# Delta rule scan: which engine spreads W and copies the state, from chunk 9 and after the last solve

## The chip, the cores and the metric

One core of a Trainium2 chip runs the whole program. The metric is the device time of one execution in microseconds; the lower, the better. TensorE multiplies matrices into PSUM, VectorE (DVE in the rows) and ScalarE (ACT) read PSUM and write SBUF, GpSimd (POOL) fills tiles and scatters rows, SyncE (SP) issues most transfers. Each engine runs its own instructions in the order in which the program issues them, and waits for another engine through semaphores.

## The reference, cut to what matters

Three stages follow each other. The first is a delta rule over 4 batches of 8 heads with 768 tokens of 48 elements; the second sends each of the 3072 resulting rows of 384 to one of 8 experts, the third is a feed-forward layer with a squared ReLU. The change lies in the first stage alone:

```python
k_n = k / (norm(k) + 1e-06)
state = zeros((B, H, D, D))
for t in range(S):
    y[:, :, t] = q_t @ state
    v_old = k_n_t @ state
    state = state + beta_t * outer(k_n_t, v_t - v_old)
```

## The kernel before, in words

**Chunks.** The 768 tokens are cut into 24 chunks of 32 (`s`, `NS = 24`), which run one after the other in the loop of `attention()`, because each needs the state that the one before left. All 32 pairs of batch and head are worked at once, as two halves `hq` of four heads times four batches. Four chunks form a group `g` of six.

**A chunk.** For each half, TensorE adds the values (`mmV`) and the keys times the state (`mm1K`) in the bank `CH[hq]`. `U(s)` spreads the result into a block-diagonal tile `Ub[hq]`: half 0 on VectorE by one multiplication of 128x768 with a mask (`blocks`), half 1 on ScalarE by four copies of 32x192. Then come the queries times the state (`mm1Q`), the transposes of the last chunk's output rows (`xrt`, copied by ScalarE), and `W`: TensorE multiplies `Ub` with the inverted triangle `TTl[g]` into columns 256 to 448 of `CH[hq]`, and the result is spread, negated, into the block-diagonal `Wb[hq]`. Half 0 goes to ScalarE as four copies (L358), half 1 to VectorE as one `blocks` (L326). `xlog` makes the router's logits. `dS` (L364) multiplies the raw keys with `Wb[hq]` into the state bank `SP_[hq]`, for half 0 and then for half 1, eight matmuls each; every one of them reads all 128 partitions of `Wb[hq]`. ScalarE copies the state of each half to `Sb[hq]` in two parts of 48x384 (L374, four a chunk). `PW` (L396) makes the output rows from both `Wb`, and ScalarE copies them to `XG` (L408).

**Order.** Nothing is scheduled by a tool: every engine gets its instructions in the order of the Python code (`manual_schedule`). The triangles are solved on VectorE, in `lanes(g)`, as a stream of some 100 short operations for each group (L271, L279, and at the end the transposes L284). `fill()` deals these out at three places of a chunk by a budget; a stream leaves `streams` when its last operation is issued. Streams 0 to 5 are due by chunks 0, 4, 8, 12, 16 and 20. The router of the rows (`route`) also runs on VectorE: `R[0]` finds the expert of each row (L446 to L466, one-hot at L455), `R[1]` are TensorE's rank counts (L460, L463), `R[2]` the slots on VectorE (L471 to L487), after which GpSimd scatters the rows (L490). For chunks 20 and 21 the router's three parts are issued at the very end of chunks 21 and 22, so `R[1]` stands on TensorE ahead of `mmV` and `mm1K` of the next chunk. In chunks 21 to 23 VectorE also rounds the first expert's weights (`pre1`, L636), after `W` and ahead of `xlog`.

**After the loop** the last rows are routed, the rows of the first expert are gathered, and the experts start, whose matmuls fill TensorE to the end.

Of the kernel before, what the change touches and what calls it, by code (L numbers as in the profile page):

```python
# [13 lines left out]
AF = mybir.ActivationFunctionType  # L14
# [8 lines left out]
def kernel(  # L23
# [17 lines left out]
    V, G, A, PE = nc.vector, nc.gpsimd, nc.scalar, nc.tensor  # L41
    NT, DM = out.shape
    D = k2.shape[-1]
    NS, C = kq.shape[0], kq.shape[-1]
# [70 lines left out]
    CH = [pp.tile([128, 512], F32, name=f"ch{i}") for i in range(2)]  # L115
    SP_ = [pp.tile([128, 512], F32, name=f"sp{i}") for i in range(2)]
# [6 lines left out]
    Wb = [wp.tile([128, 4, 4, 48], F32, name=f"Wb{i}") for i in range(2)]  # L123
    Sb = [wp.tile([128, 4, 2, 2, 48], F32, name=f"Sb{i}") for i in range(2)]
# [69 lines left out]
    def masked(g, b):  # L194
        a = PL2[g][:, b].rearrange("p s c j -> p (s c) j")
        V.tensor_tensor(a, a, mask.unsqueeze(1).broadcast_to([128, 8, C]), ALU.mult)
# [103 lines left out]
    def mmV(s, hq):  # L300

        g, i = divmod(s, 4)
        PE.matmul(
            CH[hq][:, 0:192],
            ident,
            vV[g][:, i, 4 * hq : 4 * hq + 4].rearrange("p a e -> p (a e)"),
            start=True,
            stop=s == 0,
            skip_group_check=True,
        )  # L310

    def mm1K(s, hq):
        for m in range(2):
            for b in range(4):
                PE.matmul(
                    CH[hq][C * b : C * b + C, m * 96 : m * 96 + 96],
                    KQ[s][0][:, hq * 2 + m, b],
                    Sb[hq][:, b, m].rearrange("p a e -> p (a e)"),
                    start=False,
                    stop=True,  # L320
                    skip_group_check=True,
                )

    def blocks(o, w, n):

        V.tensor_tensor(  # L326
            o,
            w.rearrange("p (x e) -> p x e", e=D).unsqueeze(2).broadcast_to([128, 4, 4, D]),
            blk[:, n].unsqueeze(1).unsqueeze(3).broadcast_to([128, 4, 4, D]),
            ALU.mult,  # L330
        )

    def U(s):
        blocks(Ub[0], CH[0][:, 0:192], 0)
        for b in range(4):
            A.activation(
                Ub[1][C * b : C * b + C, :, b, :],
                CH[1][C * b : C * b + C, 0:192].rearrange("p (a e) -> p a e", a=4),
                AF.Copy,
            )  # L340

    def W(s, hq):
        g, i = divmod(s, 4)
        for f in range(4):
            PE.matmul(
                CH[hq][C * f : C * f + C, 256:448],
                TTl[g][:, i * 8 + hq * 4 + f],
                Ub[hq][:, f].rearrange("p b e -> p (b e)"),
                start=True,
                stop=True,  # L350
            )
        if hq:
            blocks(Wb[1], CH[1][:, 256:448], 1)
            return
        for f in range(4):
            o = Wb[0][C * f : C * f + C, :, f, :]
            w = CH[0][C * f : C * f + C, 256:448].rearrange("p (b e) -> p b e", b=4)
            A.activation(o, w, AF.Copy, scale=-1.0)  # L358

    def dS(s, hq):  # L360
        g, i = divmod(s, 4)
        for b in range(4):
            for par in range(2):
                PE.matmul(  # L364
                    SP_[hq][64 * par : 64 * par + D, b * 96 : b * 96 + 96],
                    kL2[g][:, i, b * 2 + hq],
                    Wb[hq].rearrange("p b (m r) e -> p b r m e", r=2)[:, b, par],
                    start=(s == 0 and b == 0),
                    stop=(s == NS - 2),
                    skip_group_check=True,  # L370
                )
        for par in range(2):
            r = 64 * par
            A.activation(  # L374
                Sb[hq][r : r + D, :, :, par, :],
                SP_[hq][r : r + D, 0:384].rearrange("p (b m e) -> p b m e", b=4, m=2),
                AF.Copy,
            )

    def mm1Q(s):  # L380
        for p in range(4):
# [261 lines left out]
    def attention():  # L643
        streams, route_q = deque(), deque()
# [30 lines left out]
        def fill(now, part):  # L675

            nonlocal budget, lent
            pace = max(need(now), 8.0 if now < 3 else 6.6 if now < 16 else 0)
            budget += pace * part
            while streams and budget > 0 or route_q:  # L680
                if streams and budget > 0:
                    a, b = streams[0], streams[1] if len(streams) > 1 else None
                    most = pace * (due(a.g) - now)
                    c = a.pop()
                    budget -= c
                    lent += c * (most / max(a.left + c, 0.1) - 1)
                    if b is None or now < b.since or not a.ops:
                        lent = 0.0
                    if lent > 0:
                        c = b.pop()  # L690
                        lent -= c
                        budget -= c
                if route_q:
                    route_q.popleft()()
            if not streams:
                budget = 0.0
# [76 lines left out]
        for s in range(NS):  # L773
            g, i = divmod(s, 4)
            last = g == NG - 1
            while s not in ready:
                streams[0].pop()
            if s:
                mmV(s, 0)
                mmV(s, 1)  # L780
                mm1K(s, 0)
                mm1K(s, 1)
            U(s)
            fill(s, 0.25)
            if s:
                mm1Q(s)
            if s > 0:
                xT = xrt(s - 1)
            while streams and streams[0].g <= g:
                streams[0].pop()  # L790
            W(s, 0)
            W(s, 1)
            if s == NS - 1:
                lows.pop(0)()
            if s == 0:
                for b in range(4):
                    masked(0, b)
            for _ in range(2 if s > 1 else 1):
                if ahead < min(15 if s < 3 else 18 if s < 4 else NS, s + 15):
                    gram(ahead)  # L800
                    ahead += 1
            if scats and s >= E:
                drain(route_q)
                scats.pop(0)()
            fill(s + 0.25, 0.4)
            if s == NS - 4:
                first_x()
            if s >= NS - 3:
                pre1(s - NS + 3, False)
            if scats and s >= NS - 10:  # L810
                scats.pop(0)()
            if R is not None and s in (6, 10, 14, 17, 19):
                drain(route_q)
                R[1]()
                queue(R[2])
                scats += R[3]
            if s > 0:
                xlog(s - 1, xT)
                if i == 0 or s == 18:
                    R = route(g, 0, 2) if i else route(g - 1, 2 if s == 20 else 0, 4)  # L820
                    R[0][0]()
                    queue(R[0][1:])
                    if last and i == 0:
                        drain(route_q)
            if s + 1 < NS:
                dS(s, 0)
                dS(s, 1)
            if s == NS - 1:
                R = route(NG - 1, 2, 3)
                for o in R[0]:  # L830
                    o()
            PW(s)
            if last and i == 0:
                R[1]()
                queue(R[2])
                scats += R[3]
            if s <= E:
                padding(s)
            if s == 0:
                for n in range(15, 18):  # L840
                    load_kq(n)
            if i == 3 and g + 2 < NG:
                load_v(g + 2)
                load_k2(g + 2)
            if s % 3 == 2:
                for n in range(s + 16, min(s + 19, NS)):
                    load_kq(n)
            while ahead // 4 - 1 > made:
                made += 1
                streams.append(Stream(made, s + 1.6))  # L850
            fill(s + 0.65, 0.35)
            if s in (15, 17, 20):
                pre1((15, 17, 20).index(s), True)
            if s in (NS - 3, NS - 2):
                R = route(g, s - NS + 3, s - NS + 4)
                for o in R[0] + [R[1]] + R[2]:
                    o()
                scats += R[3]
# [560 lines left out]
```

## Time and profile before

| What | Value |
|---|---|
| Time, median of 3 runs | 946.1 us (945.6 to 953.18) |
| The profiled execution: its own time, and its span | 945.33 us, 943.6 us |
| PE busy | 874.4 us (93%) |
| DVE busy | 619.3 us (66%) |
| ACT busy | 449.0 us (48%) |
| POOL busy | 102.8 us (11%) |
| Mean granted TensorE clock | 0.962 |

The chunk loop takes the span from about 51 us to 257 us. The busy shares are means over the whole span, and stages with different limits lie in it. In the page's row of 40 slices VectorE stands at 8 or 9 tenths from 24 to 236 us and mostly lower in the third stage. A chunk is dated here by the end of its work on ScalarE, the copy to `XG` (L408).

### The profile page before, as it was taken

How to read it: one execution, taken by the hardware profiler on the slowest of the kernel's cores; microseconds unless marked ns; L12 is line 12 of the kernel's file. 1: busy time of each engine (PE TensorE's matmuls, PEld its weight loads, DVE VectorE, ACT ScalarE, POOL GpSimd, SP SyncE). 2: the span in 40 equal slices, each digit the busy share in tenths (PEclk: the TensorE clock that was granted, in tenths of full speed). 3: DMA queues.
4: the chain of work that ended last, by engine and by line, in shares of the span. 5: the costliest groups of instructions: out<-in, count | busy, mean ns of one | idle time of the engine just before them, and what ended most of it. 6: DMA issues, size and time to landing. Idle time of an engine off the chain costs nothing.

```text
span 943.6 us, 22357 instructions
## 1 busy us (share of the span) xinstructions
PE 874.4 (93%) x8859; PEld 787.2 (83%) x8859; DVE 619.3 (66%) x1655; ACT 449.0 (48%) x1115; POOL 102.8 (11%) x144
## 2 busy tenths in 40 slices
PE   4668889999899899998999799999999999999998
PEld 2446667667688788897987699999999999999998
DVE  6998899998668898888888592615243342516150
ACT  2245767667744666465646381514233332424150
POOL 3002013212211122212211200000000000000000
PEclk7587999999999999999999899999999999999999
DMA  8785866141245677477666550101010202020000
GB/s 332 238 264 195 241 182 186 69 148 68 75 154 167 227 259 257 151 237 241 215 216 208 154 143 17 34 17 34 17 34 9 42 9 43 9 43 1 26 1 25
DMA packets 98850, 117.80 MB, mean 125 GB/s; under 512 B 56147, under 2 KB 75706, under 8 KB 98736
## 3 DMA queue, kind: packets, MB, share of 16 engines
q1 hardware_dynamic: 90288, 89.37, 31.1%
q0 software_dynamic: 8288, 26.87, 7.7%
q8 instruction: 75, 1.23, 0.5%
q14 instruction: 39, 0.32, 0.1%
q10 hardware_dynamic: 160, 0.01, 0.0%
HBM read 84.12 MB, written 32.89 MB: 124 GB/s over the span
## 4 chain that ended last, share of the span: by engine, by line
PE 51%; issue 4%; DVE 3%; ACT 2%; DMA 1%; POOL 0%; POOLq 0%; DVEq 0%; ACTq 0%
PE gp L1129 7%; PE gp L1131 7%; PE gp L1130 7%; PE xp L1129 4%; PE xp L1131 4%; PE xp L1130 4%; PE yp L1129 3%; PE yp L1131 3%; PE yp L1130 3%; PE sp L1131 3%; PE sp L1130 3%; PE sp L1129 3%; DMA wscr<-t2k 1%; DVE wb L581 1%; ACT junk L907 1%
## 5 line engine op out<-in xcount | busy, mean ns | idle before, releaser
L1328 DVE TENSOR_TENSOR t4k<-t2k 128x384 f32<-128x384 f32 x128 | 71.3, 557 | 196.6 <-ACT t2k L1327 193.7
L1129 PE MATMUL xp<-wb,hh 128*128 128x384 f32 x184 | 62.1, 338 | 0.0
L279 DVE TENSOR_TENSOR TL<-TL,tmp 128x135 f32<-128x135 f32 (+15 forms) x186 | 60.9, 337 | 1.8
L1131 PE MATMUL xp<-wb,hl 128*128 128x384 f32 x184 | 61.9, 336 | 0.0
L1130 PE MATMUL xp<-wb,hh 128*128 128x384 f32 x184 | 61.8, 336 | 0.0
L271 DVE TENSOR_TENSOR tmp<-AL,TL 128x135 f32<-128x135 f32 (+15 forms) x186 | 60.5, 337 | 1.6
L374 ACT ACTIVATE Sb<-sp 48x384 f32<-48x384 f32 x92 | 44.7, 485 | 26.1 <-PE sp L364 24.4
L1129 PE MATMUL yp<-xh,W 128*128 128x384 f32 (+1 forms) x156 | 52.9, 339 | 1.2 <-DVE hl L1222 1.2
L1129 PE MATMUL sp<-xh,W 128*128 128x384 f32 (+1 forms) x156 | 52.8, 338 | 0.7 <-DVE hl L1222 0.5
L1131 PE MATMUL sp<-xh,W 128*128 128x384 f32 (+1 forms) x156 | 52.8, 338 | 0.5 <-DVE W L581 0.5
L1130 PE MATMUL sp<-xl,W 128*128 128x384 f32 (+1 forms) x156 | 52.7, 338 | 0.2 <-DVE xl L958 0.2
L1131 PE MATMUL yp<-xh,W 128*128 128x384 f32 (+1 forms) x156 | 52.6, 337 | 0.0
L1130 PE MATMUL yp<-xl,W 128*128 128x384 f32 (+1 forms) x156 | 52.5, 337 | 0.0
L1129 PE MATMUL gp<-wb,hh 128*128 128x384 f32 x152 | 51.4, 338 | 0.0
L1131 PE MATMUL gp<-wb,hl 128*128 128x384 f32 x152 | 51.1, 336 | 0.0
L1130 PE MATMUL gp<-wb,hh 128*128 128x384 f32 x152 | 51.1, 336 | 0.0
L1272 POOL DMA_INDIRECT x<-y,rows x32 | 34.3, 1072 | 131.5 <-ACT y L1269 74.0
L1129 PE MATMUL gp<-xh,W 128*128 128x384 f32 (+1 forms) x144 | 48.6, 337 | 0.0
L1131 PE MATMUL gp<-xh,W 128*128 128x384 f32 (+1 forms) x144 | 48.5, 337 | 0.0
L1130 PE MATMUL gp<-xl,W 128*128 128x384 f32 (+1 forms) x144 | 48.4, 336 | 0.0
L364 PE MATMUL sp<-Wb,kL 128*48 128x96 f32 x736 | 44.4, 268 | 1.3 <-DVE Wb L326 0.9
L1351 ACT ACTIVATE y<-gp 128x384 f32<-128x384 f32 x12 | 5.9, 492 | 82.8 <-PE gp L1131 82.8
(327 smaller groups left out, 2483.4 us busy)
## 6 DMA issues: line engine op xcount, KB each, us to landing
W<-in_moe_w_dram SPq DMA_DIRECT2D x42, 256.0 KB, 8.1
hb<-in_moe_w_dram SPq DMA_DIRECT2D x24, 384.0 KB, 5.3
t4k<-in_moe_w_in_dram SPq DMA_DIRECT2D x12, 512.0 KB, 4.0
t4k<-in_moe_w_out_dram SPq DMA_DIRECT2D x16, 384.0 KB, 3.3
W<-wscr SPq DMA_DIRECT2D x16, 384.0 KB, 3.9
W<-in_kq_dram SPq DMA_DIRECT2D x11, 512.0 KB, 6.4
xs<-padrow POOLq DMA_DIRECT2D x8, 693.0 KB, 7.8
xe<-xs SPq DMA_DIRECT2D x8, 594.0 KB, 7.5
```

The costliest lines, as they stand in the source:

```text
L271: V.tensor_tensor(tv[0], AL[:, j, j + 1 :].unsqueeze(1).broadcast_to([128, n, m]), T[:, :n, j : j + 1].broadcast_to([128, n, m]), ALU.mult,)
L279: V.tensor_tensor(T[:, : j + 1, j + 1 :], T[:, : j + 1, j + 1 :], tv[0], ALU.add)
L364: PE.matmul(SP_[hq][64 * par : 64 * par + D, b * 96 : b * 96 + 96], kL2[g][:, i, b * 2 + hq], Wb[hq].rearrange("p b (m r) e -> p b r m e", ...
L374: A.activation(Sb[hq][r : r + D, :, :, par, :], SP_[hq][r : r + D, 0:384].rearrange("p (b m e) -> p b m e", b=4, m=2), AF.Copy,)
L581: El.tensor_tensor(part(wt, 1, c, n), raw, hi.bitcast(F32), ALU.subtract)
L907: add(lambda t=t: A.activation(junk[:p], x[:, t, 0:DM], AF.Square, accum_out=ss[:, t : t + 1]))
L1129: PE.matmul(ps, hs, rh, start=first, stop=False)
L1130: PE.matmul(ps, hs, rl, start=False, stop=False)
L1131: PE.matmul(ps, ls, rh, start=False, stop=last)
L1272: to_x2 = lambda n=n, t=t, y=y, rows_e=rows_e: G.indirect_dma_start(out=x2, out_offset=bass.IndirectOffsetOnAxis(ap=rows_e[:n, t : t + 1]. ...
L1328: V.tensor_tensor(s2, r, r, ALU.mult)
L1351: A.activation(y, ps[:, :DM], AF.Copy)
```

## The change

`W` and `dS` take a flag. `solved` is true when no stream of solve operations is left at the point of `W`.

- Chunks 0 to 8: as before in which engine does what.
- From chunk 9, while a solve is left: both halves of W are spread by ScalarE, four copies each.
- Where no solve is left: both halves of W are spread by VectorE, one `blocks` each, and the state of half 1 is copied by VectorE (two copies of 48x384) in place of ScalarE.

```diff
-    def W(s, hq):
+    def W(s, hq, dve):
 ...
-        if hq:
-            blocks(Wb[1], CH[1][:, 256:448], 1)
+        if dve:
+            blocks(Wb[hq], CH[hq][:, 256:448], 1)
             return
         for f in range(4):
-            o = Wb[0][C * f : C * f + C, :, f, :]
-            w = CH[0][C * f : C * f + C, 256:448].rearrange("p (b e) -> p b e", b=4)
+            o = Wb[hq][C * f : C * f + C, :, f, :]
+            w = CH[hq][C * f : C * f + C, 256:448].rearrange("p (b e) -> p b e", b=4)
             A.activation(o, w, AF.Copy, scale=-1.0)
-    def dS(s, hq):
+    def dS(s, hq, dve):
 ...
         for par in range(2):
             r = 64 * par
-            A.activation(
-                Sb[hq][r : r + D, :, :, par, :],
-                SP_[hq][r : r + D, 0:384].rearrange("p (b m e) -> p b m e", b=4, m=2),
-                AF.Copy,
-            )
+            o = Sb[hq][r : r + D, :, :, par, :]
+            d = SP_[hq][r : r + D, 0:384].rearrange("p (b m e) -> p b m e", b=4, m=2)
+            if dve:
+                V.tensor_copy(o, d)
+            else:
+                A.activation(o, d, AF.Copy)
...
-            W(s, 0)
-            W(s, 1)
+            solved = not streams
+            W(s, 0, solved)
+            W(s, 1, solved or s < 9)
...
-                dS(s, 0)
-                dS(s, 1)
+                dS(s, 0, False)
+                dS(s, 1, solved)
```

## Rows read from the trace of the kernel before

**Rows 1.** Stretch view, five chunks: width, busy PE, PEld, DVE, ACT, POOL, clock

```profile
165.58:175.34 9.76, 8.11 (x139) 5.93 (x139) 9.61 (x33) 5.50 (x14) 3.45 (x5) 0.83 0.25 96
175.34:183.47 8.13, 7.74 (x145) 5.63 (x144) 8.13 (x34) 5.38 (x14) 1.95 (x2) 1.00 0.21 77
190.64:199.65 9.01, 7.98 (x139) 6.15 (x139) 8.94 (x32) 5.50 (x15) 1.95 (x2) 0.81 0.47 141
199.65:207.75 8.10, 8.04 (x145) 5.77 (x144) 7.07 (x19) 5.38 (x14) 1.05 (x2) 1.00 0.68 249
222.63:229.82 7.19, 7.19 (x147) 5.36 (x146) 7.00 (x22) 5.38 (x14) 2.25 (x3) 1.00 0.34 118
```

**Rows 2.** Timeline of chunk 19: start, length, instruction, idle before and releaser

```profile
225.43 1.34 ACT L358 ACTIVATE Wb<-ch 32x192 f32<-32x192 f32 x4
226.09 0.95 DVE L326 TENSOR_TENSOR Wb<-ch,blk 128x768 f32<-128x768 f32 x1
226.82 1.32 PEld L364 LDWEIGHTS sp<-Wb,kL 128*48 128x48 f32 x30 [0.18 <-ACT Wb L358]
227.78 2.02 ACT L374 ACTIVATE Sb<-sp 48x384 f32<-48x384 f32 x4 [1.01 <-PE sp L364]
228.27 0.48 PEld L396 LDWEIGHTS yp<-Wb,PL 128*32 128x32 f32 x16
229.91 0.65 PEld L315 LDWEIGHTS ch<-Sb,W 128*32 128x32 f32 x32 [0.23 <-issue]
230.84 1.36 ACT L336 ACTIVATE Ub<-ch 32x192 f32<-32x192 f32 x4 [0.53 <-PE ch L315]
```

**Rows 3.** Waits, 142 to 231 us: waiter, awaited, total us, times, longest

```profile
DVE Ub L326 <- PE ch L315: 1.0, 2, 0.8
PE ch L345 <- DVE Ub L326: 2.5, 3, 1.3
PE ch L345 <- DVE TTt L284: 1.6, 1, 1.6
```

**Rows 4.** Stretch view of single microseconds in chunks 12 and 15

```profile
172.00:173.00 1.00, 1.00 (x18) 1.00 (x16) 1.00 (x5) 0.37 (x1) 0.00 (x0) 0.50 0.53 203
193.00:194.00 1.00, 0.28 (x8) 0.24 (x12) 1.00 (x4) 0.51 (x2) 0.66 (x1) 1.00 1.01 424
196.00:197.00 1.00, 1.00 (x16) 1.00 (x14) 1.00 (x5) 0.00 (x0) 0.27 (x1) 0.50 0.00 0
```

**Rows 5.** Groups by line and form, 143 to 230 us: busy, mean ns

```profile
L261 DVE TENSOR_TENSOR vV<-vV,sm 128x384 f32<-128x384 f32 x12 | 6.6, 551 | 0.0
```

**Rows 6.** Timeline, end of chunk 19 to chunk 22

```profile
229.43 0.66 DVE L284 STREAM_TRANSPOSE TTt<-TL 128x256 f32<-128x256 f32 x1
231.84 0.94 PE L345 MATMUL ch<-Ub,TTt 128*32 128x192 f32 x16
233.66 0.16 PEld L364 LDWEIGHTS sp<-Wb,kL 128*48 128x48 f32 x2
234.01 1.32 PEld L364 LDWEIGHTS sp<-Wb,kL 128*48 128x48 f32 x30 [0.18 <-ACT Wb L358]
242.25 0.16 DVE L446 COPY lg<-xp 128x8 f32<-128x8 f32 x1
243.24 0.17 DVE L455 TENSOR_TENSOR oh<-iota_e,rsm 128x8 bf16<-128x8 f32 x1
243.56 0.10 PEld L460 LDWEIGHTS <-tri 128*128 128x128 bf16 x1 [0.30 <-issue]
250.79 0.10 PEld L460 LDWEIGHTS <-tri 128*128 128x128 bf16 x1 [0.30 <-issue]
```

**Rows 7.** Timeline of chunk 23

```profile
254.09 0.16 PEld L345 LDWEIGHTS ch<-Ub,TTt 128*32 128x32 f32 x8 [0.17 <-issue]
255.09 0.96 DVE L326 TENSOR_TENSOR Wb<-ch,blk 128x768 f32<-128x768 f32 x1 [1.77 <-PE ch L345]
258.24 0.17 PE L460 MATMUL xp<-oh,tri 128*128 128x8 bf16 x1 [1.24 <-DVE oh L455]
```

## The prediction

> **What bounds the kernel now.** I read the stretches chunk by chunk first, then the timeline of one undisturbed chunk, then the waits, then the clock. The stretches show VectorE busy nearly throughout: 9.61 of 9.76 us in chunk 12, 8.94 of 9.01 in chunk 15, 7.00 of 7.19 in chunk 19, while ScalarE works about 5.4 us of each [rows 1]. That looks like a loop bound by VectorE, and in some chunks it is: from 142 to 231 us TensorE waited 2.5 us for a late `Ub` of VectorE and 1.6 us for the last transpose of a solve, 4.1 us together, while VectorE itself waited 1.0 us [rows 3]. But the shortest chunk, 7.19 us, is no VectorE chain. In chunk 19 ScalarE spreads half 0 of W until 226.77; TensorE then loads dS at 226.82, PW at 228.27, `mm1K` at 229.91, and ScalarE's `Ub` begins at 230.84 [rows 2]. In that part VectorE appears nowhere: its half of W ends at 227.04, before dS has got through half 0. The loads of dS and PW follow one another without a wait, and in front of `mm1K` TensorE shows only 0.23 us of issue. So from the end of half 0 to `mm1K` the chain is TensorE's own, with ScalarE's state copies (ending at 229.80) just beside it. [...]
>
> **Chunks 9 to 19 (11 chunks).** VectorE loses one `blocks` of 0.95 us a chunk [rows 2]; ScalarE gains four copies, which take 1.34 us together [rows 2].
>
> *Cost.* ScalarE has no gap for them off the path: half 1 of W now ends 1.34 us after half 0. TensorE's eight matmuls of dS for half 0 take 16 of the 30 loads in 1.32 us, 0.70 us [rows 2], and then those of half 1 must wait 1.34 - 0.70 = 0.64 us. Behind them on TensorE, in order, stand PW, `mmV` and `mm1K`, so `Ub` comes 0.64 us later too. If instead the state copies set the end of the chunk, they begin when ScalarE is through with W, 1.34 us after half 0 rather than 1.01 us [rows 2], so that the cost is about 0.33 us. I take 0.65 us, since the trace shows no wait of TensorE for those copies longer than its own 0.23 us of issue, and half 0 of the state is done a microsecond before it is used. 11 x 0.65 = +7.2 us; by the lower end 11 x 0.35 = +3.9 us.
>
> *Gain.* VectorE's 8.94 us of chunk 15 become 8.0, its 7.00 of chunk 19 become 6.05 [rows 1]; against a chunk of 7.19 + 0.65 = 7.84 us it is no longer late. Of the 4.1 us of waiting all goes then; at the other end half, where a chunk's load is uneven. I take -4.1 us. What is late next is half 1 of W on ScalarE, the cost above.
>
> *Clock.* Chunks 12 and 13 took 17.89 us, 3.5 over twice 7.19; 1.6 of this is the transpose, so the fall cost 1.9. Chunks 15 and 16 took 17.11, 2.7 over; about 1.1 was a late `Ub`, so this fall cost 1.6 [rows 1, 3]. I price a fall at 1.75 us. Both followed a wait for VectorE of 1 us or more, and such waits go, so both falls may go (-3.5); but shorter ones, of 0.64 us, come in every chunk, and longer ones below. I take one fall in place of two: -1.75 us; ends: -3.5, and +3.5 if there are four.
>
> Sum of this part: 7.2 - 4.1 - 1.75 = +1.35 us.
>
> **Chunks 20 to 22.** The last transpose of the last solve is at 229.43 [rows 6], ahead of chunk 20's `Ub`, and the stream is then empty, so `solved` holds from chunk 20 on and not before: VectorE has solve work in every chunk up to there.
>
> *W on VectorE.* Two `blocks` of 0.96 us replace ScalarE's 1.34 us for half 0. In chunk 20 TensorE multiplies W from 231.84 for 0.94 us, both halves [rows 6]; half 0 is there at 232.31, the first `blocks` runs from about 232.4 to 233.4, half 1 to 234.3. TensorE loaded dS at 233.66 behind `xlog` and waited for ScalarE until 234.01 [rows 6], so dS begins 0.35 us earlier and half 1 is there as half 0 ends: -0.35 us. No ScalarE work follows that would be in the way.
>
> *Copies of the state on VectorE.* Two for half 1. No row shows such a copy; 384 elements took 0.55 us in an SBUF product [rows 5], 0.50 on ScalarE [rows 2]. I take 0.5 us each, bounds 0.4 and 0.6. The state itself is not late, since `mm1K` of half 1 comes after half 0. What comes behind them on VectorE is. In chunks 21 and 22 the router's operations L446 to L455 stand behind the copies, and TensorE's rank count L460 waits for the one-hot L455, with `mmV` and `mm1K` of the next chunk behind it. Before, these ran while ScalarE copied: L446 at 242.25, L455 ending at 243.41, rank count at 243.56 [rows 6]. From the end of dS's loads to the rank count it was then 0.91 us, all TensorE's own: 0.13 to PW, 0.48 of PW, 0.30 of issue [rows 2, 6]. Now it is 0.2 us of handing over, 0.95 of copies, 1.16 from L446 to the end of L455, and 0.15 to TensorE, 2.46 us. With dS 0.35 us earlier, 2.46 - 0.91 - 0.35 = +1.2 us, in chunk 21 and, by the same order (rank count at 250.79 [rows 6]), in chunk 22. Ends: with copies of 0.4 us each 0.2 less a chunk, with 0.6 us 0.2 more; and if the 0.35 us by which dS begins earlier does not come, as much more. In chunk 20 the one-hot is issued ahead of dS, so it costs nothing there.
>
> Sum: -0.35 + 1.2 + 1.2 = +2.05 us, between +1.6 and +3.5.
>
> [...]
>
> **Chunk 23.** No dS. VectorE's single `blocks` ran at 255.09 after 1.77 us of idling; behind it the low parts, weights and router ran without a gap to the rank count at 258.24, which waited for L455 [rows 7]. TensorE loads W's half 0 at 254.09 [rows 7] and needs half of 0.94 us for it, so the first `blocks` begins about 254.6 and half 1 ends near 256.45 instead of 256.05: +0.4 us (0 to +1) for all that follows.
>
> **Sum.** 1.35 + 2.05 + 0.4 = +3.8 us. After the loop everything waits for the last routed rows, so the shift is passed on: 945.33 + 3.8 = 949.1 us. The profiled execution lies 0.8 us below the median of the runs, within what I can tell; I predict 949.0 us.
>
> **Rivals.**
>
> *Relief of VectorE wins.* ScalarE's copies and not TensorE set the chunk's end, and the clock no longer falls: 3.9 - 4.1 - 3.5 + 2.45 = -1.25 us, 944.1 us; with the router's wait halved and no cost in chunk 23, about 942.5 us. For it: VectorE's saturation [rows 1]. Against it: the 0.23 us of issue ahead of `mm1K` and no wait for the copies [rows 2]. Chance 0.28.
>
> *The clock falls throughout (slower).* TensorE now waits 0.64 us between the halves of dS in each of 11 chunks and over a microsecond for the rank count in two. Without any fall the sum is 945.33 + 7.2 - 4.1 + 2.45 = 950.9, less 3.5, 947.4 us; each fall adds 1.75. From five falls on, 956.1 us, it is slower by over 1%; with one in every second of the 14 chunks 959.6 us. For it: two of the waits of about a microsecond or more were followed by a fall [rows 3, 4]. Against it: chunk 19 and its like have short waits in every step and a full clock [rows 1]. [...] Chance 0.08.
>
> *The change does not do what it says.* If `solved` came late or never, chunks 20 to 23 would get ScalarE's version: 945.33 + 1.35 + 4 x 0.65 = 949.3 us. The transposes' place [rows 6] speaks against it. Chance 0.02.
>
> *More than 1% faster.* That takes 9.5 us: all waits and both falls are 7.6 us, chunks 20 to 22 at best 1 us, so only an effect that I don't see could bring it. Chance 0.03.
>
> **How the numbers follow.** The forecast has the remaining 0.59. About 1% is what a measurement of this kernel can tell from no change. Forecast, relief and the rival without effect all lie within 1% of 946.1 (936.6 to 955.6): 0.59 + 0.28 + 0.02 = 0.89; slower 0.08; faster 0.03. The range goes from 942, the relief at its best, to 955, the forecast with two more falls and the upper ends of the router's wait and chunk 23; outside lie the falls throughout and the tails, some 0.15.
>
> **What would show it.** In chunks 9 to 19: undisturbed chunks of about 7.85 us, VectorE idle in front of `Ub` for `mm1K`, and a wait of about 0.64 us of TensorE's dS for ScalarE's W. If these chunks are 7.5 us, the state copies set the end. In chunk 20 dS about 0.3 us earlier. At the ends of chunks 21 and 22 the rank count waiting for L455 by more than a microsecond, with the copies L374 (now VectorE's) ahead of L446. Wrong would be: chunks 9 to 19 still waiting for a late `Ub`; a clock granted at 0.50 in more than two of them; or a loop that ends later with a span that does not, which would mean that what follows waits for something else.

## The result and the profile after

The changed kernel takes 956.24 us (median of 20 runs, 952.8 to 964.74), the kernel before 951.04 us (20 runs, 945.6 to 955.19). The ratio is 1.0067 [1.0049, 1.0085]: slower, by about 6.3 us, where I had forecast 3.8 us more and a time of at most 955. The median of the three runs shown with the kernel before (946.1 us) and its profiled execution (945.33 us) lie at the low end of its 20 runs; in later batches of 12 and more runs its median was 948.4 to 949.4 us. The profiled execution of the changed kernel (956.31 us, span 954.6 us) is 11 us longer, more than the ratio says; what belongs to the change is read from stretches of the loop, which repeat from one execution to the next.

I cut these stretches where ScalarE starts its first copy of `Ub` (L336 in both) in a chunk; "stretch 14" runs from that of chunk 14 to that of chunk 15. In the table, 23 to experts runs on to the first rounded `hh` of the experts.

| us | 9 to 20 | 20 to 23 | 23 to experts | experts to end |
|---|---|---|---|---|
| before | 87.38 | 22.21 | 17.95 | 672.60 |
| before, a second profile (e5) | 87.41 | 21.83 | 19.27 | 676.21 |
| after | 90.27 | 24.91 | 19.42 | 675.58 |

The loop is 2.9 us longer up to chunk 20 and 2.7 to 3.1 us longer in chunks 20 to 22. The last column differs by 3.6 us between two executions of one kernel, so the 3 us there are no finding.

The stretch view (width, busy PE, PEld, DVE, ACT, POOL with their counts, clock, DMA share, GB/s), first all of chunks 9 to 19 of before:

```profile
143.46:230.84 87.38, 82.60 (x1673) 62.17 (x1666) 85.25 (x286) 60.43 (x158) 19.10 (x20) 0.96 0.38 122
```

Then after. The first row is again all of chunks 9 to 19. The next three run from one copy to `XG` (L409) to the next, as in [rows 1]: the second and fourth are undisturbed chunks and answer to chunk 19 of before, the third is one with a gap, of which more below. The last two are, roughly, chunks 21 and 22.

```profile
144.42:234.69 90.27, 87.01 (x1665) 61.45 (x1668) 75.78 (x275) 74.11 (x203) 20.66 (x21) 1.00 0.35 112
...
175.05:183.03 7.98, 7.75 (x143) 5.37 (x143) 7.97 (x34) 6.67 (x18) 2.72 (x3) 1.00 0.14 53
191.01:200.03 9.02, 8.29 (x143) 5.57 (x143) 7.49 (x23) 6.67 (x19) 1.95 (x2) 1.00 0.44 138
225.15:233.13 7.98, 7.80 (x148) 5.53 (x148) 6.11 (x21) 6.67 (x19) 1.09 (x2) 1.00 0.38 119
240.00:248.80 8.80, 6.79 (x144) 5.11 (x144) 6.78 (x23) 3.54 (x9) 2.37 (x2) 1.00 0.13 48
248.80:258.00 9.20, 7.57 (x146) 5.86 (x146) 6.76 (x25) 3.76 (x9) 0.97 (x1) 1.00 0.07 26
```

VectorE is busy for 75.78 of 90.27 us, where it had 85.25 of 87.38 before. An undisturbed chunk takes 7.98 us instead of 7.19, whether VectorE is busy for 7.97 of it or for 6.11; the granted clock is 1.00. The timeline of chunk 19 of after (start, length, instruction, idle before and its releaser; lines have moved, L364 is still dS, the state copies are L379 on ScalarE and L377 on VectorE, PW is L397) answers to [rows 2]:

```profile
228.33 2.73 ACT L358 ACTIVATE Wb<-ch 32x192 f32<-32x192 f32 x8
229.73 0.66 PEld L364 LDWEIGHTS sp<-Wb,kL 128*48 128x48 f32 x14 [0.18 <-ACT Wb L358]
230.77 0.16 PEld L364 LDWEIGHTS sp<-Wb,kL 128*48 128x48 f32 x2 [0.38 <-ACT Wb L358]
231.09 2.02 ACT L379 ACTIVATE Sb<-sp 48x384 f32<-48x384 f32 x4
231.11 0.66 PEld L364 LDWEIGHTS sp<-Wb,kL 128*48 128x48 f32 x14 [0.18 <-ACT Wb L358]
231.91 0.48 PEld L397 LDWEIGHTS yp<-Wb,PL 128*32 128x32 f32 x16
233.54 0.65 PEld L315 LDWEIGHTS ch<-Sb,W 128*32 128x32 f32 x32 [0.23 <-issue]
234.69 1.36 ACT L336 ACTIVATE Ub<-ch 32x192 f32<-32x192 f32 x4 [1.07 <-PE ch L315]
```

The eight copies of W run for 2.73 us, TensorE has done half 0 of dS at 230.39 and waits until 231.06 for the last copy, here shown as two waits of 0.38 and 0.18 with two early loads between. Behind it dS, PW, `mmV` and `mm1K` follow one another. The state copies end at 233.11, 0.43 us before `mm1K`, which again shows only 0.23 us of issue. `Ub` comes 1.15 us after `mm1K` here; in the undisturbed chunks of after it is 1.00 us.

The waits of after from 142 to 264 us (waiter, awaited, total us, times, longest) answer to [rows 3]:

```profile
DVE Ub L326 <- PE ch L315: 16.0, 12, 2.2
PEld sp L364 <- ACT Wb L358: 6.7, 26, 0.4
PE xp L461 <- DVE oh L456: 3.3, 2, 1.6
PEld yp L384 <- issue: 1.6, 4, 0.6
PE ch L345 <- DVE TTt L284: 0.3, 1, 0.3
```

VectorE, which waited 1.0 us for `mm1K` before, now waits 16.0 us (15.4 of them up to 235 us, about where [rows 3] end), and up to chunk 20 TensorE waits for VectorE hardly at all. In its place stand ScalarE's W, the one-hot, and a line I had not expected, 1.6 us of issue in the middle of `mm1Q` (L384).

Chunk 21 of after in the timeline answers to chunk 21 in [rows 6] (router L447 to L456, rank count L461):

```profile
244.63 1.33 PEld L364 LDWEIGHTS sp<-Wb,kL 128*48 128x48 f32 x32
245.60 0.99 ACT L379 ACTIVATE Sb<-sp 48x384 f32<-48x384 f32 x2 [1.79 <-PE sp L364]
246.20 1.12 DVE L377 COPY Sb<-sp 48x384 f32<-48x384 f32 x2 [0.37 <-PE sp L364]
246.87 0.10 PEld L461 LDWEIGHTS <-tri 128*128 128x128 bf16 x1 [0.30 <-issue]
248.35 0.17 DVE L456 TENSOR_TENSOR oh<-iota_e,rsm 128x8 bf16<-128x8 f32 x1
248.57 0.17 PE L461 MATMUL xp<-oh,tri 128*128 128x8 bf16 x1 [1.63 <-DVE oh L456]
257.38 0.17 PE L461 MATMUL xp<-oh,tri 128*128 128x8 bf16 x1 [1.63 <-DVE oh L456]
```

TensorE is ready for the rank count at 246.94 and gets the one-hot at 248.57, because VectorE's two copies, which end at 247.32, stand ahead of the router. The same 1.63 us come in chunk 22 (last row). And chunk 23, beside [rows 7], with both spreads of W on VectorE:

```profile
261.17 1.82 DVE L326 TENSOR_TENSOR Wb<-ch,blk 128x768 f32<-128x768 f32 x2 [1.35 <-PE ch L345]
265.18 0.17 PE L461 MATMUL xp<-oh,tri 128*128 128x8 bf16 x1 [1.60 <-DVE oh L456]
```

### The profile page after: what moved, and what is told of

It is laid out like the page before. It is cut to its first block, busy times and chain, and to the rows that moved or that the text cites. A ratio compares the mean times of both kernels' runs of the same rounds, so it can differ in the third digit from the quotient of the medians.

```text
span 954.6 us, 22366 instructions
## 1 busy us (share of the span) xinstructions
PE 882.0 (92%) x8859; PEld 788.9 (83%) x8859; DVE 617.5 (65%) x1654; ACT 455.2 (48%) x1137; POOL 103.7 (11%) x144
## 4 chain that ended last, share of the span: by engine, by line
PE 53%; DVE 5%; issue 4%; ACT 3%; DMA 2%; POOL 0%; SPq 0%; DVEq 0%; ACTq 0%; POOLq 0%
PE gp L1131 7%; PE gp L1133 7%; PE gp L1132 7%; PE xp L1131 4%; PE xp L1133 4%; PE xp L1132 4%; PE yp L1131 3%; PE yp L1133 3%; PE yp L1132 3%; PE sp L1132 3%; PE sp L1133 3%; PE sp L1131 3%; ACT junk L909 1%; DMA wscr<-t2k 1%; DVE wb L582 1%
## 5 line engine op out<-in xcount | busy, mean ns | idle before, releaser
L364 PE MATMUL sp<-Wb,kL 128*48 128x96 f32 x736 | 48.0, 265 | 2.5 <-ACT Wb L358 1.8
L379 ACT ACTIVATE Sb<-sp 48x384 f32<-48x384 f32 x86 | 41.7, 485 | 16.7 <-PE sp L364 14.7
```

The lines of the kernel that those rows point to most:

```text
L364: PE.matmul(SP_[hq][64 * par : 64 * par + D, b * 96 : b * 96 + 96], kL2[g][:, i, b * 2 + hq], Wb[hq].rearrange("p b (m r) e -> p b r m e", ...
L379: A.activation(o, d, AF.Copy)
```

## The experiments

Twelve kernels. My theory after the result: in chunks 9 to 19 TensorE's wait for ScalarE costs more than the relief of VectorE brings, and in chunks 21 and 22 VectorE's copies delay the one-hot. Stretches of all of them:

| us | 9 to 20 | 20 to 23 | ratio to before |
|---|---|---|---|
| e1, W in chunks 9 to 19 alone | 90.63 | 22.56 | 1.0048 [1.0016, 1.0079] |
| e2, the end alone | 87.50 | 24.82 | 1.0046 [1.0021, 1.0071] |
| e3, one-hot first | 90.91 | 21.47 | 1.0034 [1.0006, 1.0063] |
| e4, values between the halves of dS | 86.73 | 26.88 | 1.0033 [1.0007, 1.0060] |
| e5, the kernel before again | 87.41 | 21.83 | 1.0012 [0.9992, 1.0032] |
| e6, e3 and e4 together | 84.80 | 21.24 | 0.9971 [0.9950, 0.9992] |
| e7, e2 and e3 together | 86.95 | 21.04 | 1.0011 [0.9990, 1.0032] |
| e8, relief in six chunks, e3 | 83.02 | 21.04 | 0.9962 [0.9937, 0.9988] |
| e9, ScalarE in chunks 17 to 19 | 89.89 | 21.79 | one run, 950.14 us beside 949.43 |
| e10, e8 with chunk 23 as before | 82.97 | 21.04 | 0.9941 [0.9915, 0.9968] |
| e11, scatters later | 89.94 | 24.31 | one run, 953.09 us beside 954.12 |
| e12, no scatters in chunks 9 to 19 | 87.86 | 24.70 | one run, 949.65 us beside 954.12 |

### The two parts by themselves

**e1: only the W of chunks 9 to 19.**

```diff
-            W(s, 0, solved)
+            W(s, 0, False)
...
-                dS(s, 1, solved)
+                dS(s, 1, False)
```

> Only the part of chunks 9 to 19: ScalarE spreads both halves of W; chunks 20 to 23 as before the change. Theory (TensorE's dS of half 1 waits for ScalarE): the stretch from Ub of chunk 9 to Ub of chunk 20 on ScalarE takes about 90 us as in the changed kernel (90.3) against 87.4 before, undisturbed chunks 7.98 us; chunks 20 to 23 as before (Ub of 20 to Ub of 23 22.2 us); the time lies about 2 to 3 us over the kernel before. Rival (the loss is all in chunks 20 to 23): within 1 us of the kernel before, or faster by a few us, if its clock falls are not matched by the waits.

**e2: only the part behind the last solve.**

```diff
-            W(s, 1, solved or s < 9)
+            W(s, 1, True)
```

> Only the part behind the last solve: from chunk 20 both halves of W and half of the state on VectorE; chunks 9 to 19 as before the change. Theory (rank count behind the state copies): Ub of chunk 20 to Ub of chunk 23 takes 24.9 us as in the changed kernel against 22.2 before, the rank count waits about 1.6 us for the one-hot in chunks 21 and 22, and the time lies 3 to 4 us over the kernel before, since the stretch after the loop loses too. Rival (the loss is all in chunks 9 to 19): within 1 us of the kernel before.

Each part alone costs, by ratio 0.48% and 0.46%, and each shows its cost in its own stretch: e1 90.63 us up to chunk 20, e2 24.82 us behind it. The two together make 0.94% where the whole change made 0.67%, which the intervals allow. The relief, bought with that wait, is no gain.

e2 also told something that I was not looking for. Its chunks 9 to 19 are those of the kernel before, and no clock fell in them; they take 87.50 us, as in the two profiles of before with two falls each. The stretch view of e2 over chunks 9 to 19:

```profile
142.97:230.47 87.50, 78.36 (x1674) 59.90 (x1669) 86.13 (x293) 61.07 (x158) 16.23 (x19) 1.00 0.35 113
```

The granted clock is 1.00, and VectorE is busy for 86.13 us. The waits of e2 from 142 to 230 us:

```profile
PE ch L345 <- DVE Ub L326: 7.2, 8, 1.7
PE ch L345 <- DVE TTt L284: 1.6, 1, 1.6
```

TensorE waits 7.2 us for VectorE's `Ub` where it had waited 2.5 us [rows 3]. What a low clock took in the one execution, waiting for VectorE takes in the other: VectorE's work sets these 87.4 us.

### Taking the new waits away

**e3: the one-hot ahead of the state copies in chunks 21 and 22.**

```diff
+            if s in (NS - 3, NS - 2):
+                R = route(g, s - NS + 3, s - NS + 4)
+                for o in R[0]:
+                    o()
             if s + 1 < NS:
                 dS(s, 0, False)
...
-                R = route(g, s - NS + 3, s - NS + 4)
-                for o in R[0] + [R[1]] + R[2]:
+                for o in [R[1]] + R[2]:
```

> The changed kernel, but in chunks 21 and 22 the router's first part (through the one-hot) is issued ahead of dS, so that on VectorE it stands ahead of the copies of the state. Theory: the rank count no longer waits, Ub of chunk 20 to Ub of chunk 23 falls from 24.9 to about 21 us (three chunks like the 6.84 us of chunk 20), and the time falls by 3 to 4 us against the changed kernel. Rival (the copies themselves, or W on VectorE, are what is late): the chunks stay above 8 us and the time within 1 us of the changed kernel.

Chunks 20 to 22 fall from 24.91 to 21.47 us. The timeline of chunk 21 of e3 shows the order and no wait at the rank count:

```profile
246.88 0.17 DVE L456 TENSOR_TENSOR oh<-iota_e,rsm 128x8 bf16<-128x8 f32 x1
247.10 0.17 PE L461 MATMUL xp<-oh,tri 128*128 128x8 bf16 x1
247.10 1.11 DVE L377 COPY Sb<-sp 48x384 f32<-48x384 f32 x2
```

So the wait was the whole cost of that part, and the copies themselves, which now come later still, cost nothing.

**e4: `mmV` of half 0 for the next chunk between the halves of dS, in chunks 9 to 19.**

```diff
+        early = set()
...
-                mmV(s, 0)
+                if s not in early:
+                    mmV(s, 0)
...
                 dS(s, 0, False)
+                if 8 < s < 20 and s + 1 in ready:
+                    mmV(s + 1, 0)
+                    early.add(s + 1)
                 dS(s, 1, solved)
```

> The changed kernel, but in chunks 9 to 19 TensorE is given mmV of the next chunk's half 0 between the two halves of dS, where it waits for ScalarE's second half of W. Theory (TensorE's serial chain sets the chunk): some 0.4 us of each wait is filled, undisturbed chunks fall from 7.98 to about 7.55 us, and the stretch of chunks 9 to 19 by about 4.5 us. Rival (ScalarE, with W and the state copies behind one another, sets the chunk): chunks stay at 7.9 to 8.0 us and the time within 1 us of the changed kernel.

The rival here was that ScalarE's copies set the chunk, so that filling TensorE's wait would bring nothing. A chunk falls from 7.98 to 7.65 us, 0.1 us less of a fall than I had expected. The timeline of chunk 19 of e4:

```profile
223.23 0.66 PEld L364 LDWEIGHTS sp<-Wb,kL 128*48 128x48 f32 x14 [0.18 <-ACT Wb L358]
224.02 0.30 PEld L303 LDWEIGHTS ch<-vV,ident 128*128 128x128 f32 x2
224.54 0.73 PEld L364 LDWEIGHTS sp<-Wb,kL 128*48 128x48 f32 x16 [0.23 <-issue]
224.59 2.02 ACT L379 ACTIVATE Sb<-sp 48x384 f32<-48x384 f32 x4
226.71 0.65 PEld L315 LDWEIGHTS ch<-Sb,W 128*32 128x32 f32 x32 [0.23 <-ACT Sb L379]
```

`mmV` (L303) sits in the wait, and half 1 of dS follows without a wait for ScalarE. Now `mm1K` starts 0.10 us after the end of the state copies and is put down to them; in after it started 0.43 us behind them. In the kernel before the two were level as well: `mm1K` started 0.11 us after the copies in most chunks, and the waits of its weight loads from 142 to 231 us, beside [rows 3], put 9 of 11 down to the copies:

```profile
PEld ch L345 <- DVE Ub L326: 3.9, 6, 1.5
PEld ch L315 <- ACT Sb L374: 2.0, 9, 0.2
```

In chunk 21 of this execution of e4 the granted clock was 0.50 from 242.7 to 246.1, behind the wait for the one-hot that e4 keeps and that was 2.29 us long here; that stretch took 10.90 us instead of 8.85. A single microsecond of e4 there, in the stretch view:

```profile
243.00:244.00 1.00, 1.00 (x6) 1.00 (x4) 0.72 (x7) 0.00 (x0) 0.00 (x0) 0.50 0.00 0
```

**e5: the kernel before, unchanged**, as a measure of what executions differ by.

> The kernel before, unchanged, in another execution. If the 3 us that the changed kernel's profile loses behind the first expert's first copy (675.6 against 672.6 us) and the 1 us ahead of chunk 9 belong to the execution and not to the change, this trace shows about 675 us there too, and the loop still 87 to 88 us from Ub of chunk 9 to that of chunk 20. If they belong to the change, it shows 672 to 673 us.

The granted clock fell twice again, at 158.7 to 162.1 and 175.8 to 179.2 us, in other chunks than before (171.6 to 175.0, 195.5 to 198.9); it was 0.50 from 160 to 162 us, as in [rows 4]. The eleven chunks took 87.41 us, where before had 87.38.

**e6: e3 and e4 in one kernel.**

> The changed kernel with both mends: the one-hot ahead of the state copies in chunks 21 and 22, and mmV of the next chunk's half 0 between the halves of dS in chunks 9 to 19. If the two losses are separate and these are all of them: 86.7 us from chunk 9 to 20 (87.4 before), 21.5 from chunk 20 to 23 (22.2 before), and the time within 2 us of the kernel before. If the rest of the loss lies elsewhere: 3 us or more above it.

Faster than before, 945.09 us against 948.42 (0.9971), and more so than I expected (within 2 us). With the one-hot's wait gone and the other partly filled, the change is a gain. But the 84.80 us up to chunk 20 are not to be booked to the two mends alone: in these chunks e6 has the code of e4, which took 86.73 us. e4 lost most of the difference in stretches 17 and 19 (8.49 and 8.23 us), where a scatter of GpSimd fell on the start of `mm1K`; in e6 a scatter at the same place, 0.36 us after `mm1K` of chunk 18, did nothing. The timelines of the two at chunk 18, e4 first (what such a gap is comes below):

```profile
210.93 0.98 POOL L491 DMA_INDIRECT xs<-XG,sloti  x1 [4.04 <-ACT Sb L379]
212.24 0.32 PEld L384 LDWEIGHTS yp<-Sb,W 128*32 128x32 f32 x12 [0.53 <-issue]
...
212.15 0.98 POOL L491 DMA_INDIRECT xs<-XG,sloti  x1 [3.75 <-ACT Sb L379]
212.40 0.71 PEld L384 LDWEIGHTS yp<-Sb,W 128*32 128x32 f32 x32
```

**e7: e2 with e3's order.**

> Chunks 9 to 19 as before the change; from chunk 20 the changed version with the one-hot ahead of the state copies. Theory: the part behind the last solve is then a gain, 21.5 us from chunk 20 to 23 against 22.2, 87.5 in chunks 9 to 19, and the time 0 to 1.5 us under the kernel before, which is no measurable difference. Rival (VectorE's copies of W and state cost of themselves): 24 us and 3 us over.

No difference that can be measured. The stretch of chunks 20 to 22 is 0.8 to 1.2 us shorter than before, but in the profiled execution the clock behind the loop was low for some 7 us (weight loads of 128x128 in float32 took 0.33 us) and 23 to experts took 20.09 us, so one profile cannot show it in the end.

### Where relief pays

**e8: ScalarE takes half 1 of W only in chunks 10 to 15, with `mmV` between; e3's order.**

```diff
-            W(s, 1, solved or s < 9)
+            W(s, 1, solved or not 9 < s < 16)
...
+                if 9 < s < 16 and s + 1 in ready:
```

> ScalarE spreads half 1 of W only in chunks 10 to 15, where VectorE has 7.9 to 8.9 us of work a chunk, with mmV between the halves of dS there; chunks 9 and 16 to 19 as before the change; behind the last solve as in the changed kernel with the one-hot first. Theory (before the change VectorE's amount of work sets chunks 9 to 19, 85 of 87.4 us, and TensorE's wait sets them after it): about 83 us from chunk 9 to 20 and 21.5 from 20 to 23, the time 4 to 5 us under the kernel before. Rival (chunks before are set by single late operations and falls of the clock, not by VectorE's amount): 86 to 88 us, no difference.

**e9: the opposite, ScalarE only in chunks 17 to 19, nothing else of the change.**

```diff
-            W(s, 0, solved)
-            W(s, 1, solved or s < 9)
+            W(s, 0, False)
+            W(s, 1, solved or s < 17)
...
-                dS(s, 1, solved)
+                dS(s, 1, False)
```

> The kernel before, but ScalarE spreads both halves of W in chunks 17, 18 and 19 alone, where VectorE has only 6.7 to 7.2 us of work a chunk and was not late; all else as before. Theory (TensorE's wait for the second half is a cost of its own, the relief of VectorE is worth nothing where VectorE is not late): these three chunks take 7.98 us each instead of 7.47, 7.43 and 7.19 of the other run of the kernel before, together about 1.9 us more, and the chunks ahead stay as they were. Rival (the cost comes with the whole row of chunks): they stay at 7.2 to 7.5 us.

e9's stretches 17 to 19 take 8.13, 7.96 and 7.96 us, 24.05 together, against 7.47, 7.43 and 7.19 (22.09) in e5: where VectorE is hardly late, the wait is all loss, 0.65 us a chunk. e8 has 83.02 us up to chunk 20: in the chunks with most solve work 7.65 us, later 7.2 to 7.4. That answers e8's rival, by which single late operations and clock falls set these chunks: it would have left 86 to 88 us. e9 and e10 ran on another chip than e1 to e8; their times stand beside the kernel before on that chip.

**e10: e8 with chunk 23 as before.**

```diff
-            W(s, 0, solved)
+            W(s, 0, solved and s < NS - 1)
```

> The selected version (ScalarE spreads half 1 of W in chunks 10 to 15, mmV between the halves of dS there, the one-hot ahead of the state copies), with half 0 of W in chunk 23 on ScalarE as before the change. Theory: the rank count behind the loop comes about 0.4 us earlier, the stretch from Ub of chunk 23 to the first expert's first copy takes 18.1 to 18.2 us instead of 18.57 with one fall of the clock in it (17.95 before with one); the time stays 4 to 5 us under the kernel before. Rival (VectorE's two spreads in chunk 23 cost nothing): 18.5 to 18.6 us.

The timeline of chunk 23 of e10, beside after's above:

```profile
250.68 0.96 DVE L326 TENSOR_TENSOR Wb<-ch,blk 128x768 f32<-128x768 f32 x1 [1.05 <-PE ch L345]
253.84 0.17 PE L461 MATMUL xp<-oh,tri 128*128 128x8 bf16 x1 [1.32 <-DVE oh L456]
```

The rank count comes 5.31 us after `Ub` instead of 5.77 in e8. The shorter stretch that I expected behind it did not show, 19.45 us: the clock was low from 254.7 to 261.5 in this execution (weight loads of 128x128 in float32 took 0.33 us, 0.19 behind it); in e8 it was low for 3.4 us and the stretch took 18.57. With 942.64 us against 949.43, 0.9941 [0.9915, 0.9968], e10 beats the kernel before; that chunk 23 adds to e8's gain is not shown by the times, whose intervals overlap.

### The gaps inside `mm1Q`

Eleven chunks of 7.98 us are 87.8, but after has 90.27, because stretches 14, 15 and 17 took 9.02, 8.62 and 8.52 us. In each, TensorE stops in the middle of `mm1Q`, and `Ub` comes 0.5 to 1 us late. The timeline of after at chunks 15 and 18, one pair of scatter and gap each:

```profile
191.98 0.97 POOL L491 DMA_INDIRECT xs<-XG,sloti  x1 [9.26 <-ACT XG L409]
193.30 0.30 PEld L384 LDWEIGHTS yp<-Sb,W 128*32 128x32 f32 x10 [0.58 <-issue]
193.46 1.36 ACT L336 ACTIVATE Ub<-ch 32x192 f32<-32x192 f32 x4 [1.96 <-PE ch L315]
...
217.07 0.98 POOL L491 DMA_INDIRECT xs<-XG,sloti  x1 [8.31 <-ACT Sb L379]
218.35 0.43 PEld L384 LDWEIGHTS yp<-Sb,W 128*32 128x32 f32 x17 [0.34 <-issue]
```

TensorE takes up its loads 1.32 and 1.28 us after GpSimd's scatter of rows (L491) began; the third pair (200.60 and 201.88) gives 1.28. e1 and e3 have the gaps in the same chunks and with the same distance. That could be the scatter, or the place in TensorE's instruction stream, which is the same in the three kernels.

**e11: six small GpSimd copies ahead of every scatter.**

```diff
         def scat(i):
+            for _ in range(6):
+                G.tensor_copy(late, si[:, i : i + 1].broadcast_to([128, 64]))
             G.indirect_dma_start(
```

> The changed kernel with six small GpSimd copies (64 columns of the slot numbers each) in front of every scatter, so that each scatter starts some 1.2 to 1.6 us later. In the changed kernel the chunks 14, 15 and 17 take 9.02, 8.62 and 8.52 us instead of 7.98, and in each of them TensorE takes up its loads again 1.25 to 1.32 us after a scatter's start, the scatter having started 0.03 to 0.56 us after mm1K. Theory 'scatter': the gaps go from those three chunks (7.98 to 8.1 us each), and chunks whose scatter started 1.2 to 1.5 us ahead of mm1K (12, 16, 18) may get one of 0.3 to 0.6 us. Rival 'place in the instruction stream': the gaps stay in chunks 14, 15 and 17 at 8.5 to 9.0 us, and chunks 9 to 19 take 90.3 us as before.

Stretches 15 and 17 are 7.97 us now, and 16 and 18, whose scatters moved onto the start of `mm1K`, are 8.59 and 8.87. The timeline of e11 at chunk 17:

```profile
205.28 0.65 PEld L315 LDWEIGHTS ch<-Sb,W 128*32 128x32 f32 x32 [0.23 <-issue]
205.39 0.98 POOL L494 DMA_INDIRECT xs<-XG,sloti  x1 [0.62 <-ACT XG L409]
206.70 0.36 PEld L384 LDWEIGHTS yp<-Sb,W 128*32 128x32 f32 x16 [0.44 <-issue]
```

Again 1.31 us after the scatter. The gaps moved with the scatters and not with the instructions. Two details differ: stretch 12 got no gap, as in this execution its scatter fell 1.8 us ahead of `mm1K`, and stretch 14 kept 8.39 us. There a scatter started at 182.41, after `mm1Q`, and ScalarE waited for TensorE's transposes until 183.76, 1.35 us later; that this is the same stop at another place is argued, not shown.

**e12: no scatters in chunks 9 to 19.**

```diff
             if scats and s >= E:
                 drain(route_q)
-                scats.pop(0)()
+                o = scats.pop(0)
+                if not 8 < s < 20:
+                    o()
...
             if scats and s >= NS - 10:
-                scats.pop(0)()
+                o = scats.pop(0)
+                if not 8 < s < 20:
+                    o()
...
```

What is left out here makes one GpSimd transfer, in chunk 20, fill the rows that the experts read with padding.

> The changed kernel without the scatters of chunks 9 to 19 (the rows of those tokens are not handed to the experts, and their output rows are padding instead). Theory 'scatter': no issue gap of TensorE inside mm1Q in these chunks, each of them 7.97 to 8.15 us, chunks 9 to 19 together 87.9 to 88.3 us instead of 90.27. Rival 'place in the instruction stream': the gaps stay in chunks 14, 15 and 17, about 90.2 us. Rival 'DMA load': the big loads of v, k and weights cause them, which stay here: about 90.2 us too.

87.86 us, no gap. Two of its stretches, the second with transfers that keep the queues 56% busy:

```profile
177.28:185.24 7.96, 7.73 (x142) 5.36 (x141) 7.74 (x32) 6.65 (x19) 0.00 (x0) 1.00 0.01 2
201.18:209.14 7.96, 7.73 (x142) 5.36 (x142) 6.51 (x21) 6.65 (x19) 0.00 (x0) 1.00 0.56 226
```

The big loads are still there, so it is not they. The scatters cost after 2.4 us in these chunks (90.27 - 87.86), by one profile of each. e12's time and its other columns are not comparable, since the experts get other rows.

## Why the prediction was wrong

The forecast's mechanism held, its level and its sum did not. By its steps:

- **The level, the larger part of the miss.** The sum stands on 945.33 us, one execution, which I took to lie 0.8 us below the median of three runs. The 20 runs have a median of 951.04, 5.7 us higher. The same +3.8 us on that would have given 954.8, just inside the range; the forecast was 7.2 us short, and the other 1.4 us (by the difference of the medians, 5.2) or 2.5 (by the ratio, 6.3) are the sum's.
- **Cost in chunks 9 to 19: right in kind, undersized.** TensorE's dS waits for ScalarE's half 1 of W. A chunk went from 7.19 to 7.98 us, 0.79 instead of my 0.65: from half 0 of W to PW it took 2.23 us instead of 1.50 (ScalarE's eight copies in one line take 2.73 us), and from `mm1K` to ScalarE's `Ub` 1.00 instead of 0.93. 11 x 0.79 = +8.7 against +7.2. In rival "relief wins" the state copies were to set the chunk; in after they end 0.43 us ahead of `mm1K`, and filling TensorE's wait shortens the chunk (e4), so it was TensorE's. The 0.23 us that I took for issue in one chunk of before are put down to the copies in most of its chunks; this has no part in the miss.
- **Gain and clock: the first step of the sum that failed.** I priced a late VectorE by TensorE's waits (-4.1) and the clock separately (-1.75, one of two falls gone). They are the same backlog. No run shows that a fall in these chunks costs 1.75 us: e2 has none and takes 87.50 us, before and e5 have two and take 87.38 and 87.41. All that lay above 11 x 7.19 = 79.1 us was VectorE's, 8.3 us, and all of it went: -8.3 against -5.85. Even the waits were read short: those of the matmuls [rows 3] are 4.1 us, those of the weight loads in the same stretch 3.9 (above) and 1.9. Without a disturbance the part would have come to +0.4 or +0.5 us, as e12 shows (87.86 - 87.4).
- **What the sum had no term for: the second.** Scatters that started beside `mm1K` stopped TensorE: +2.4 us (e12). Before had two as well (scatter at 207.68, `Ub` 1.35 us after `mm1K` instead of 0.93), but there VectorE's work set the length of the eleven chunks: 87.38 us with the two stops, 87.41 in e5 and 87.50 in e2 without any. With that backlog gone, nothing covers the scatters. So +1.35 became +2.9: 1.5 more of cost, 2.45 more of gain, and 2.4 of scatters. How many of after's 20 runs have such stops no profile shows.
- **Chunk 20: right.** -0.47 us (6.84 for 7.31), forecast -0.35.
- **Rank count in chunks 21 and 22: right in place, undersized.** Stretches of 8.85 and 9.22 us for 7.24 and 7.66, +1.6 each where I had +1.2. The larger part is the gain that I took off: dS was to begin 0.35 us earlier, but its loads end 4.42 and 4.38 us after ScalarE's `Ub` instead of 4.49, only 0.1 us earlier (4.01 in chunk 20). The rest is the copies, 0.56 us each (the sum has 0.95 for both); the first began 0.24 us after the end of dS's loads, at 246.20. e3 removes all of it. A state copy took 0.56 us on VectorE and 0.495 on ScalarE in chunk 21 (L377 and L379 above).
- **Chunk 23: right.** The rank count waits 1.60 us instead of 1.24 [rows 7]; e10 gets 0.46 us back.
- **The clock rival.** The waits of some 0.55 us in each of eleven chunks (0.38 and 0.18 above) brought no fall in chunks 9 to 19 of after (granted clock 1.00), e1 or e3 (the 16 weight loads of PW took 0.48 us in each of these chunks; in chunk 12 of before, at the low clock, 0.84). Nor did the waits of 1.6 us for the one-hot in chunks 21 and 22 of after, e2, e11 and e12. Only the one of 2.29 us in chunk 21 of e4 was followed by a fall, to 0.50 from 242.7 to 246.1; with the longer wait itself it cost 2 us. That its length made the difference is not shown.

The parts add to +2.9, +2.7 and +0.4, 6.0 us by the first profile of before, near the 6.3 of the ratio. That sum is from single profiles; the ratio's interval is 4.7 to 8.1 us.

## What to carry to other kernels

Where an engine is late in some chunks only, waits and clock falls of the others can be two faces of one backlog, as here (87.38 us with 2.5 us of waits for `Ub` and two falls in before, 87.50 with 7.2 and none in e2): compare the total of the stretch with the minimum chunk times their number, and don't book both. Moving work off the late engine paid in those chunks (e8, 83.02 us up to chunk 20 for 87.4) and cost in the others (e9, 0.65 us a chunk), and filling the wait for the new owner with independent work gave 0.33 us a chunk back (e4). Put a forecast on the median of many runs: here the level was off by as much as the effect. Ahead of an operation that is moved to another engine's queue, look for the small operation behind it that a third engine waits for, and issue that first (e3, 3.4 us in chunks 20 to 22).

## What the runs showed that I had not expected

**A scatter can stop TensorE.** I took all 14 profiles (before, after and the twelve kernels), and in each the chunks 9 to 22, 196 in all. ScalarE's `Ub` starts 0.93 to 1.0 us after `mm1K` where nothing disturbs it. In 25 chunks a scatter of GpSimd started between 0.2 us before and 0.7 us after `mm1K`; in 18 of them `Ub` came 1.29 to 2.04 us after `mm1K`. One of the 18 (chunk 22 of e4) is the low clock's doing, its loads show no gap; the other 17 are stops. Of the other 171 chunks none had `Ub` later than 1.25 us. Where the gap shows in the loads of `mm1Q`, TensorE resumed 1.25 to 1.32 us after the scatter's start. That the scatter is the cause is shown by e11 and e12. It is not enough by itself: the 17 all lie in before, after, e1, e3, e4 and e11, and there every scatter so placed but the one under the low clock stopped TensorE; the 7 without harm all lie in e6 to e10, on two chips, and there none did. e2, e5 and e12 had no scatter so placed. What sets such executions apart, and what in the scatter stops TensorE, stays open; comparisons across the two groups (e4 with e6) carry the stops as well.

**The low clock behind the loop lasts 3.4 or 6.8 us**, in kernels of either kind: before 260.4 to 263.8, e8 254.2 to 257.6, but e5 254.3 to 261.1 and after 264.7 to 271.6. A weight load of 128x128 in float32 took 0.33 us there and 0.19 behind it, in all four. A row of after there, in the stretch view, with a granted clock of 0.50:

```profile
266.00:268.00 2.00, 1.42 (x8) 1.31 (x7) 1.97 (x6) 0.49 (x1) 0.87 (x1) 0.50 0.00 0
```

It goes with 23 to experts at 17.95 to 18.58 us (before, e8, e6) or at 19.27 to 19.45 us (e5, after, e10), so a single profile cannot tell a change of half a microsecond there.
